# Four unused tiles between the buffers of a chunk's split activations

## The chip, the cores and the metric

The kernel runs on one core of a Trainium2 chip. The metric is device time in microseconds (us) for one execution, and the figure given for a kernel is the median of its runs. Five engines work side by side: TensorE (PE in the profile, with its weight loads listed apart as PEld), VectorE (DVE), ScalarE (ACT), GpSimd (POOL) and SyncE (SP), which issues DMAs. A tile on the chip has 128 partitions; where this text gives a tile's size or place in bytes, it means bytes in one partition.

## The reference

The reference is a light convolution followed by a feed-forward layer that keeps a maximum in place of an activation. `x` is (8, 4160, 192), the filters are (8, 4160, 8, 7), and the three up weights are (192, 768) each; the output has 33,280 rows of 192.

```python
w = exp(weight_gen - max); w = w / (sum(w) + 1e-9)       # over the 7 taps, for each head
x_unf = x_pad[:, s + k, :]                                # the last 7 rows up to s
attn = einsum('bshk,bskhg->bshg', w, x_unf)               # 8 heads of 24 columns
h = maximum(maximum(attn @ w1, attn @ w2), attn @ w3)     # 192 -> 768
out = h @ w_out                                           # 768 -> 192
```

Everything is float32 in the reference. The kernel multiplies tiles of type F32R on TensorE and keeps the precision by splitting each operand into a high part and a low part.

## The kernel before, in words

**Chunks and ticks.** The 33,280 rows are cut into 65 chunks of 512 (`TC` = 4 blocks of 128). A chunk takes 22 ticks of the main loop (L636 to L667). Ticks 0 to 11 are six up steps, ticks 12 to 15 are the down product of the chunk before, one block of 128 rows a tick, and ticks 16 to 21 are the last three up steps. Work for later chunks (loads, softmax, convolution, transpose, splitting) is put on a plan by tick (`PRODUCTS`, `SUMS`, `TRANSPOSE`, `PARTS`, `SOFTMAX`, `LOAD`, and for the first ticks `OPENING`). Every instruction is pinned in the order in which the code issues it (`pin`, L178), so the order on each engine is written out by hand.

**Convolution.** For each block, POOL multiplies 7 rows by their filters (L246), and DVE sums over the taps (L261). A chunk's 512 rows are then transposed: the first three chunks on TensorE (L276, L277), the others by DVE in blocks of 32 x 32 (L284) and 24 small copies on ACT (L290) into the tile `room`.

**Splitting the activations.** `parts` (L293) makes a chunk's four moving operands, all of 128 x 512 elements. Columns 0 to 127 of the 192 become `xa_hi` (ACT, L300) and the remainder `xa_lo` (POOL, or DVE for the first three chunks, L304). Columns 128 to 191 fill 64 partitions only, so `xc` holds their high part twice, once in each half of the partitions (ACT, L306), and `xb` holds the high part in partitions 0 to 63 (ACT, L308) and the low part in 64 to 127 (POOL or DVE, L309). These steps run at ticks 13 to 15 of the chunk before.

**Up product.** A step takes one of three weight matrices `i` and a pair `jp` of 128-column groups, first the even group and then the odd one (`odd`). The matmuls (L329) are cut into two halves of the partitions, 0 to 63 and 64 to 127, which TensorE works on together: each half has its own weight load and matmul, and a small model (`advance_upper`, L427) decides where the upper half's instructions go between the lower half's. Per half and step there are nine matmuls of 512 columns: `xa_hi`, `xa_lo` and again `xa_hi` with `wa_hi`, `wa_hi` and `wa_lo`, `xb` with `wb_hi`, for both groups, and `xc` with `wb_lo` for one of them. Nine steps make 81 matmuls per half and chunk.

**Maximum.** The first of the three results is copied by ACT from PSUM to `m` (L376), the others are compared by DVE (L378). ACT then makes `h_hi` (L381) and POOL `h_lo` (L385).

**Down product.** For each block of 128 rows and each of six groups `j`, the weights of TensorE are the slices of `h_hi` and `h_lo`, and the moving operand is `wo`: 384 columns (high and low part of `w_out`) with `h_hi`, then 192 columns with `h_lo`. That is 24 pairs per half and chunk. ACT and DVE add the two parts (L410, L411), and SP stores the chunk.

**Where tiles lie.** A pool lays its tiles out in the order in which each name is first asked for, all buffers of a name side by side, and the pools follow each other in the order of L155 to L161. Worked out from the tiles' sizes, with the place that the change's own words give for `xa_hi`, the tiles that matter here start as follows (modulo 2048):

| tile | bytes x buffers | start modulo 2048 |
|---|---|---|
| `wa_hi`, `wb_hi` | 9216 x 1 each | 640 |
| `wa_lo` | 9216 x 1 | 1664 |
| `wb_lo` | 4608 x 1 | 1664 |
| `wo` | 9216 x 1 | 128 |
| `room` | 9216 x 1 | 640 |
| `xa_hi`, `xa_lo`, `xb`, `xc` | 2048 x 2 each | 1664 |
| `h_hi`, `h_lo` | 12288 x 2 each | 1664 |
| `m` | 2048 x 4 | 1664 |
| `raw_a` (raw weights, opening) | 6144 x 1 | 1152 |

Slices `wa_hi[:, j, i]` that follow each other in `i` start 512 bytes apart, in `j` 1536 bytes apart; a slice of `h_hi` for one block of rows starts 512 bytes after the block before; a slice of `wo` starts 1536 bytes after the `j` before. During the opening the buffers of `h_hi` and `h_lo` also hold raw weights (L501 to L514), and `room` holds the raw `w_out` (L515).

Of the kernel before, what the change touches and what calls it, by code (L numbers as in the profile page):

```python
# [13 lines left out]
F32 = mybir.dt.float32  # L14
# [7 lines left out]
P = 128  # L22
# [76 lines left out]
def lightconv_maxout_kernel(  # L99
# [58 lines left out]
    xtp = ctx.enter_context(tc.tile_pool(name="xtp", bufs=2))  # L158
# [19 lines left out]
    def pin(ins):  # L178

        tc.keep_in_program_order(ins)  # L180
        return ins
# [111 lines left out]
    def parts(c):  # L293

        pa, pb = state.pop(("p", c))
        xa_hi = xtp.tile([P, CH], F32R, name="xa_hi")
        xa_lo = xtp.tile([P, CH], F32R, name="xa_lo")
        xb = xtp.tile([P, CH], F32R, name="xb")
        xc = xtp.tile([P, CH], F32R, name="xc")
        pin(nc.scalar.copy(xa_hi, pa))  # L300
        yield

        eng, at = (nc.vector, halves[0]) if c < ON_TENSOR else (nc.gpsimd, halves[1])
        pin(eng.tensor_tensor(xa_lo, pa, xa_hi.bitcast(F32), op=ALU.subtract))  # L304
        for h in halves:
            pin(nc.scalar.copy(xc[h], pb))  # L306
        yield
        pin(nc.scalar.copy(xb[:DB], xc[:DB].bitcast(F32)))  # L308
        pin(eng.tensor_tensor(xb[DB:], pb, xc[at].bitcast(F32), op=ALU.subtract))  # L309
        state["xT", c] = xa_hi, xa_lo, xb, xc  # L310
# [290 lines left out]
    def finish(name):  # L601
# [6 lines left out]
        "+": total,  # L608
        "t": transpose,
        "p": parts,  # L610
        "a": prepare_a,
        "b": prepare_b,
# [92 lines left out]
```

## Time and profile before

| what | value |
|---|---|
| median of 3 runs | 1697.91 us (1697.88 to 1699.43) |
| the profiled execution's own time | 1699.39 us |
| its span, first to last instruction | 1697.6 us |
| mean granted TensorE clock | 0.998 |
| busy: PE / PEld / DVE / ACT / POOL | 1657.2 / 1466.1 / 1124.6 / 1145.8 / 1426.2 us |
| HBM read / written | 51.25 / 25.56 MB |

A row of a group in the profile gives line, engine, operation, output `<-` inputs, shapes and count, then busy microseconds and mean nanoseconds of one instruction, then the engine's idle time just before such instructions with what ended it. In a timeline a row gives start and duration in us; "x2" means that two like instructions started there. The duration of a matmul includes its way through a pipeline and overlaps the next one, so the pace of matmuls is read from the distance of their starts.

### The profile page before, as it was taken

The page shows a single profiled execution, that of the slowest core. Times are in us where ns is not written, and L with a number is a line of the kernel's source. Part 1 is how long each engine was busy: PE and PEld are TensorE (multiplying, and loading weights), DVE is VectorE, ACT ScalarE, POOL GpSimd, SP SyncE. Part 2 cuts the span into 40 slices and gives each one's busy share as a digit, 9 for nine tenths or more (in the row PEclk, how much of TensorE's full clock was granted, in tenths as well). Part 3 has the DMA queues.
Part 4 walks back from the last instruction along what each step waited for, and adds up shares of the span by engine and source line. Part 5 has one row for each costly group of instructions (what it writes and reads, how often), then busy time and mean ns, then how long its engine had stood idle before and what let it go on. Part 6 is the DMA issues. An engine that isn't in the chain of part 4 may idle for free.

```text
span 1697.6 us, 42191 instructions
## 1 busy us (share of the span) xinstructions
PE 1657.2 (98%) x16794; PEld 1466.1 (86%) x16794; DVE 1124.6 (66%) x1552; ACT 1145.8 (67%) x2896; POOL 1426.2 (84%) x844
## 2 busy tenths in 40 slices
PE   3899999999999999999999999999999999999999
PEld 2598889889889889889988988988988988988998
DVE  7966766666666666666666666666666666666653
ACT  5657667667666766766766766766776776676672
POOL 6888888989888888888888888988888888888872
PEclk9999999999999999999999999999999999999999
DMA  7010101101010110101010110101011010101000
GB/s 236 1 70 10 70 29 52 70 20 60 20 70 15 66 70 21 60 21 70 11 70 21 60 70 20 61 20 70 11 70 61 27 63 20 70 11 46 20 11 29
DMA packets 20422, 79.51 MB, mean 47 GB/s; under 512 B 2320, under 2 KB 5128, under 8 KB 17536
## 3 DMA queue, kind: packets, MB, share of 16 engines
q1 hardware_dynamic: 20104, 76.54, 11.9%
q8 instruction: 131, 2.15, 0.5%
q14 instruction: 67, 0.55, 0.1%
q10 hardware_dynamic: 120, 0.28, 0.0%
HBM read 51.25 MB, written 25.56 MB: 45 GB/s over the span
## 4 chain that ended last, share of the span: by engine, by line
PE 94%; DVE 3%; ACT 1%; DMA 1%; POOL 1%; SPq 0%; issue 0%; DVEq 0%
PE ph L329 94%; DVE acc L261 1%; DVE m L378 0%; DMA wt<-in_weight_gen_dram 0%; DVE ph L483 0%; POOL r L246 0%; DVE ph L488 0%; DVE e L495 0%; DVE ph L481 0%; DVE ph L494 0%; DMA xt<-in_x_dram 0%; SPq L529 0%; ACT room L290 0%; SPq L521 0%; POOL h_lo L385 0%
## 5 line engine op out<-in xcount | busy, mean ns | idle before, releaser
L246 POOL TENSOR_TENSOR r<-xt,wt 128x1344 f32<-128x1344 f32 x260 | 721.4, 2814 | 0.6 <-DMA xt<-in_x_dram 0.4
L378 DVE TENSOR_TENSOR m<-ph,m 128x512 f32<-128x512 f32 x780 | 520.6, 685 | 197.4 <-PE ph L329 113.7
L329 PE MATMUL ph<-xa_hi,wa_hi 64*128 64x512 f32 x2340 | 630.8, 391 | 9.4 <-DVE m L378 3.1
L385 POOL TENSOR_TENSOR h_lo<-m,h_hi 128x512 fp32r<-128x512 f32 x390 | 503.3, 1301 | 161.7 <-ACT h_hi L381 157.0
L329 PE MATMUL ph<-xa_lo,wa_hi 64*128 64x512 f32 x2340 | 626.9, 388 | 1.0 <-DVE xa_lo L304 1.0
L329 PE MATMUL ph<-xa_hi,wa_lo 64*128 64x512 f32 x2340 | 626.1, 387 | 1.1 <-POOL wa_lo L498 1.1
L329 PE MATMUL ph<-xb,wb_hi 64*128 64x512 f32 x2340 | 626.0, 387 | 0.0
L329 PE MATMUL ph<-wo,h_hi 64*128 64x384 f32 x3120 | 595.5, 355 | 0.0
L329 PE MATMUL ph<-wo,h_lo 64*128 64x192 f32 x3120 | 522.3, 247 | 0.0
L381 ACT CAST h_hi<-m 128x512 fp32r<-128x512 f32 x390 | 241.8, 621 | 409.7 <-DVE m L378 406.6
L261 DVE TENSOR_REDUCE acc<-r 128x192 f32<-128x1344 f32 x260 | 401.8, 1547 | 125.5 <-POOL r L246 125.5
L290 ACT COPY room<-room 32x128 f32<-32x128 f32 x1488 | 440.8, 296 | 25.7 <-DVE room L284 7.5
L329 PE MATMUL ph<-xc,wb_lo 64*128 64x512 f32 x1170 | 453.1, 387 | 0.1
L329 PEld LDWEIGHTS ph<-wo,h_lo 64*128 64x128 f32 x3120 | 398.8, 188 | 2.5
L329 PEld LDWEIGHTS ph<-wo,h_hi 64*128 64x128 f32 x3120 | 398.4, 184 | 2.9 <-issue 0.4
L329 PEld LDWEIGHTS ph<-xa_hi,wa_hi 64*128 64x128 f32 x2340 | 338.7, 185 | 53.9 <-DVE m L378 3.9
L329 PEld LDWEIGHTS ph<-xa_hi,wa_lo 64*128 64x128 f32 x2340 | 338.4, 185 | 42.0 <-POOL wa_lo L498 1.5
L329 PEld LDWEIGHTS ph<-xa_lo,wa_hi 64*128 64x128 f32 x2340 | 338.7, 185 | 38.7 <-DVE xa_lo L304 1.5
L329 PEld LDWEIGHTS ph<-xb,wb_hi 64*128 64x128 f32 x2340 | 338.7, 185 | 38.4 <-ACT xb L308 0.3
L376 ACT COPY m<-ph 128x512 f32<-128x512 f32 x390 | 221.8, 586 | 38.5 <-PE ph L329 35.3
L411 DVE TENSOR_TENSOR o<-ph,ob 128x192 f32<-128x192 f32 x260 | 86.7, 353 | 234.5 <-ACT ob L410 234.5
L329 PEld LDWEIGHTS ph<-xc,wb_lo 64*128 64x128 f32 x1170 | 216.3, 185 | 20.9 <-POOL wb_lo L498 0.5
(54 smaller groups left out, 702.6 us busy)
## 6 DMA issues: line engine op xcount, KB each, us to landing
xt<-in_x_dram SPq DMA_DIRECT2D x20, 1728.0 KB, 7.1
out_dram<-o SPq DMA_DIRECT2D x64, 384.0 KB, 2.3
wt<-in_weight_gen_dram SPq DMA_DIRECT2D x21, 336.0 KB, 3.0
h_hi<-in_moe_w_dram SPq DMA_DIRECT2D x6, 256.0 KB, 4.8
xt<-in_x_dram SPq DMA_DIRECT2D x1, 1536.0 KB, 9.3
h_lo<-in_moe_w_dram SPq DMA_DIRECT2D x6, 192.0 KB, 4.8
room<-in_moe_w_out_dram SPq DMA_DIRECT2D x1, 1152.0 KB, 8.1
xt<-in_x_dram SPq DMA_DIRECT2D x1, 960.0 KB, 5.2
```

What stands on the lines that cost most here:

```text
L246: nc.gpsimd.tensor_tensor(r.rearrange("p (h g) k -> p k h g", g=G), xt[:, la + t : la + t + K].rearrange("p k (h g) -> p k h g", g=G), wt[ ...
L261: nc.vector.tensor_reduce(state["acc", c][:, t], r, axis=AX.X, op=ALU.add)
L290: pin(nc.scalar.copy(to[:, :, p : p + 32], blocks[p : p + 32, :, f : f + 32]))
L329: ins = nc.tensor.matmul(ph[:, :n], w[h], v[h], start=begins and half == 0 and q == 0, stop=ends and half == 1 and q == len(terms) - 1,)
L376: pin(nc.scalar.copy(m[:, :N], ph[:, :N]))
L378: pin(nc.vector.tensor_tensor(m[:, :N], ph[:, :N], m[:, :N], op=ALU.max))
L381: later(1, lambda: pin(nc.scalar.copy(hi, m[:, :N])))
L385: nc.gpsimd.tensor_tensor(lo, m[:, :N], hi.bitcast(F32), op=ALU.subtract)
L411: pin(nc.vector.tensor_tensor(o[:, t], po[:, :D], ob, op=ALU.add))
```

## The change

In `parts`, and for the first chunk only, four tiles are asked for that nothing writes or reads. They come from the same pool, one after each of the four operands:

```diff
         xa_hi = xtp.tile([P, CH], F32R, name="xa_hi")
+        if c == 0:
+            xtp.tile([P, 64], F32, name="gap0", bufs=1)
         xa_lo = xtp.tile([P, CH], F32R, name="xa_lo")
+        if c == 0:
+            xtp.tile([P, 80], F32, name="gap1", bufs=1)
         xb = xtp.tile([P, CH], F32R, name="xb")
+        if c == 0:
+            xtp.tile([P, 96], F32, name="gap2", bufs=1)
         xc = xtp.tile([P, CH], F32R, name="xc")
+        if c == 0:
+            xtp.tile([P, 16], F32, name="gap3", bufs=1)
         pin(nc.scalar.copy(xa_hi, pa))
```

The gaps are 256, 320, 384 and 64 bytes, each with one buffer. The starts of `xa_hi`, `xa_lo`, `xb` and `xc` modulo 2048 become 1664, 1920, 192 and 576, with both buffers of each name at the same one. All that is laid out behind them (`h_hi`, `h_lo`, `m`, `o`, `ob` and the tiles of the preparation) lies 1024 bytes further on. No instruction is added, removed or moved in the code.

## The prediction

> **What bounds the kernel now.** I read the page first, then the chain of waits, then TensorE's timeline. The page:
>
> ```profile
> span 1697.6 us, 42191 instructions
> ...
> PE 1657.2 (98%) x16794; PEld 1466.1 (86%) x16794; DVE 1124.6 (66%) x1552; ACT 1145.8 (67%) x2896; POOL 1426.2 (84%) x844
> ...
> PE 94%; DVE 3%; ACT 1%; DMA 1%; POOL 1%; SPq 0%; issue 0%; DVEq 0%
> ```
>
> TensorE's matmuls are the chain for 94% of the span. Busy shares alone would not prove that, since pipelined matmuls always look busy, so the chain in order of time and the busy time by stretch come next.
>
> ```profile
> 84.35 68.39 PE ph L329 x636
> ...
> 170.18 1523.98 PE ph L329 x14710
> ...
> 1694.19 0.33 ACT ob L410
> ```
>
> ```profile
> 170.00:424.00 254.00, 253.82 (x2596) 225.87 (x2598) 168.51 (x228) 175.28 (x447) 222.24 (x130) 1.00 0.13 50
> ...
> 1186.00:1440.00 254.00, 254.00 (x2602) 226.05 (x2600) 168.07 (x226) 175.17 (x448) 219.64 (x128) 1.00 0.11 42
> ```
>
> Up to 170 us the chain changes engines (weight splitting on DVE, a first run of matmuls, one late preparation). From 170.18 us to 1694.16 us it is one unbroken run of matmuls on L329, at a granted clock of 1.00. (Columns of the last two rows: stretch, length, then busy us of PE, PEld, DVE, ACT, POOL, clock, DMA share, GB/s.) POOL, the next busiest, is idle for 254.00 - 219.64 = 34.4 us of such a stretch, or 3.4 us a chunk.
>
> The chunk's length is read from the first down matmul of a chunk. It alone lasts 0.33 us, so it is easy to find:
>
> ```profile
> 184.61 0.33 PE L329 MATMUL ph<-wo,h_hi 64*128 64x384 f32 x1
> ...
> 209.80 0.33 PE L329 MATMUL ph<-wo,h_hi 64*128 64x384 f32 x1
> ...
> 1645.43 0.33 PE L329 MATMUL ph<-wo,h_hi 64*128 64x384 f32 x1
> ...
> 1670.62 0.33 PE L329 MATMUL ph<-wo,h_hi 64*128 64x384 f32 x1
> ```
>
> 209.80 - 184.61 = 25.19 us, 1670.62 - 1645.43 = 25.19 us, and (1670.62 - 184.61) / 59 chunks = 25.19 us. So all of them have one period. It splits into two rates:
>
> ```profile
> 801.13 0.39 PE L329 MATMUL ph<-xa_hi,wa_hi 64*128 64x512 f32 x2
> 801.36 0.39 PE L329 MATMUL ph<-xa_lo,wa_hi 64*128 64x512 f32 x2
> 801.58 0.39 PE L329 MATMUL ph<-xb,wb_hi 64*128 64x512 f32 x2
> 801.81 0.39 PE L329 MATMUL ph<-xa_hi,wa_lo 64*128 64x512 f32 x1
> ...
> 803.17 0.39 PE L329 MATMUL ph<-xa_hi,wa_hi 64*128 64x512 f32 x2
> ...
> 805.21 0.39 PE L329 MATMUL ph<-xa_hi,wa_hi 64*128 64x512 f32 x2
> ...
> 817.09 0.36 PE L329 MATMUL ph<-wo,h_hi 64*128 64x384 f32 x2
> 817.28 0.25 PE L329 MATMUL ph<-wo,h_lo 64*128 64x192 f32 x2
> 817.37 0.36 PE L329 MATMUL ph<-wo,h_hi 64*128 64x384 f32 x2
> ...
> 818.51 0.36 PE L329 MATMUL ph<-wo,h_hi 64*128 64x384 f32 x2
> ```
>
> "x2" means that both row halves started that matmul together. An up step is nine matmuls per half and takes 805.21 - 803.17 = 2.04 us, or 0.2267 us a matmul; the duration column (0.39) overlaps the next matmul and is not the pace. A down pair (384 and 192 columns) takes (818.51 - 817.09) / 5 = 0.284 us. Nine steps and 24 pairs are 9 x 2.04 + 24 x 0.284 = 25.18 us: the whole period, with nothing left for waits.
>
> **The change part by part.** The four `gap` tiles have no reader or writer. They add no instruction, wait or DMA, and the instructions that remain are pinned in program order. So the number of instructions stays 42191, and the only thing that can change a time is where tiles lie. Three groups move.
>
> First, the moving operands. Before, xa_hi, xa_lo, xb and xc all start at 1664 modulo 2048, since each buffer is 2048 bytes. After it xa_hi stays and the others start at 1920, 192 and 576. Their matmuls are these:
>
> ```profile
> L329 PE MATMUL ph<-xa_hi,wa_hi 64*128 64x512 f32 x2340 | 630.8, 391 | 9.4 <-DVE m L378 3.1 <-ACT xa_hi L300 2.8 <-DVE e L495 1.7
> L329 PE MATMUL ph<-xa_lo,wa_hi 64*128 64x512 f32 x2340 | 626.9, 388 | 1.0 <-DVE xa_lo L304 1.0
> L329 PE MATMUL ph<-xa_hi,wa_lo 64*128 64x512 f32 x2340 | 626.1, 387 | 1.1 <-POOL wa_lo L498 1.1
> L329 PE MATMUL ph<-xb,wb_hi 64*128 64x512 f32 x2340 | 626.0, 387 | 0.0
> ...
> L329 PE MATMUL ph<-xc,wb_lo 64*128 64x512 f32 x1170 | 453.1, 387 | 0.1
> ```
>
> Per half that is (4 x 2340 + 1170) / 2 = 5265 matmuls, 81 a chunk. One nanosecond on each would be 5.3 us. The trace already varies the places against each other. The weight slice of a step moves by 512 bytes with i and by 1536 with j, so its start goes through 640, 1152, 1664 and 128 modulo 2048 while the moving operand stays at 1664; step after step takes 2.04 us all the same. And while the lower half reads wo, whose slices lie 1536 bytes apart (128, 1664, 1152, 640), the upper half still reads xa_hi to xc:
>
> ```profile
> 814.45 0.25 PE L329 MATMUL ph<-wo,h_lo 64*128 64x192 f32 x1
> 814.51 0.39 PE L329 MATMUL ph<-xa_hi,wa_hi 64*128 64x512 f32 x1
> ...
> 816.32 0.39 PE L329 MATMUL ph<-xa_hi,wa_lo 64*128 64x512 f32 x1
> ```
>
> That is eight of the upper half's matmuls in 1.81 us, 0.226 us each, against 0.2267 us when both halves read the same place. So I take nothing for breaking up the common place. What the trace does not hold is a moving operand whose start is not 128 modulo 512; the new ones are 384, 192 and 64. That is the bound left open on both sides, priced under the rivals.
>
> Second, what ACT, DVE and POOL do on those tiles and on what lies behind them. The gaps add 256 + 320 + 384 + 64 = 1024 bytes, so h_hi and h_lo go from 1664 to 640, and m, o, ob and the preparation tiles shift by 1024 as well. h_hi's 512-byte slices pass through the same four starts as before.
>
> ```profile
> L381 ACT CAST h_hi<-m 128x512 fp32r<-128x512 f32 x390 | 241.8, 621 | 409.7 <-DVE m L378 406.6
> ...
> L300 ACT CAST xa_hi<-room 128x512 fp32r<-128x512 f32 x62 | 38.5, 621 | 1.5
> ...
> L385 POOL TENSOR_TENSOR h_lo<-m,h_hi 128x512 fp32r<-128x512 f32 x390 | 503.3, 1301 | 161.7 <-ACT h_hi L381 157.0
> ...
> L304 POOL TENSOR_TENSOR xa_lo<-room,xa_hi 128x512 fp32r<-128x512 f32 x62 | 80.5, 1298 | 25.2 <-ACT xa_hi L300 25.2
> ...
> L476 ACT COPY f<-h_hi 128x512 uint16<-128x512 uint16 x6 | 3.7, 613 | 0.0
> ...
> L476 ACT COPY f<-raw_a 128x512 uint16<-128x512 uint16 x3 | 1.8, 614 | 0.0
> ```
>
> The first pair reads from 1664 (m) and from 640 (room), 621 ns both; the second likewise, 1301 and 1298 ns; the third from 1664 (h_hi) and 1152 (raw_a), 613 and 614 ns. Three nanoseconds at most, so zero. What covers these steps if that is wrong:
>
> ```profile
> 797.65 1.29 POOL L309 TENSOR_TENSOR xb<-room,xc 64x512 fp32r<-64x512 f32 x1
> ...
> 802.49 0.39 PE L329 MATMUL ph<-xb,wb_hi 64*128 64x512 f32 x1
> ```
>
> The chunk starts six up steps before its first down matmul at 814.28 us, at 802.04 us, and reads xb third. xb was ready at 798.94 us, so 3.5 us of matmuls cover it. POOL's write would have to take nearly four times as long before TensorE waited; past that point every microsecond would be paid 65 times.
>
> Third, the opening. Weight splitting on DVE and ACT works from 1024 bytes further on, before 170 us, on the chain. At the 1 ns by which L476 differs between places, 18 splits of about nine operations are 0.2 us either way. The sum over all three is 0.0 us within 0.2.
>
> The Trainium skill speaks against any effect: its page "SBUF — State Buffer", section "Door 1: The DMA port swizzle (why `[64,N]` ≈ `[32,N]`)", has the banks that the compute engines see made of four partitions each, so an offset along the partition changes no bank. The constant 2.04 us agrees for the starts that occur here.
>
> The profiled execution took 1699.39 us, 1.8 us more than its span of 1697.6 and 1.5 us above the median of the three runs (1697.91, range 1.55). With a sum of zero, the profiled execution stays at 1699.4 and the median at 1697.9. I call 0.2%, 3.4 us, what can be told from no change.
>
> **The rivals.**
>
> *The four operands hinder each other at one place, and spreading them helps.* For it: all four do start at the same place, and in an up step the halves often read different ones of them. Against it: the rows at 814.51 and 816.32. The timeline shows the steps of 801.13 to 801.81 as 0.23, 0.22 and 0.23 us. If every matmul took the shorter value, a step would be 9 x 0.22 = 1.98 us, 0.06 less, and 9 x 65 steps would save 35 us: 1663 us. It decides from 3.4 / 5265 = 0.65 ns a matmul. "TensorE: Matmul & The Clock Gate", section "Back-to-back issue gap", in the Trainium skill gives N / 2.4 + 2.5 ns, which is 215.8 ns for 512 columns; an estimate with that pace would save 10.9 x 5265 = 57 us, or 1640 us, and nothing here shows such a pace.
>
> *xb and xc, now at odd multiples of 64 bytes, are read more slowly.* Every moving operand before starts at a multiple of 128 (1664 = 13 x 128); 192 and 576 do not. If such a start costs each matmul as much as the longer value shown, 0.23 against 0.2267 us, the 3.3 ns fall on (2340 + 1170) / 2 = 1755 matmuls per half: 5.8 us, 1703.7 us. It decides from 3.4 / 1755 = 1.9 ns a matmul. For it: no row has such a start, and in this chain nothing would hide it. Against it: nothing in the rows varies with a start at all.
>
> *The change doesn't do what it says.* An unused tile could be given no room, or lie elsewhere. Then the program is the one before, at 1697.9 us, which this trace can't tell from my forecast.
>
> **How the numbers follow.** No effect (with the third rival in it): 0.79. Helped by spreading: 0.11, as the halves and the weights contradict it, while starts other than 128 modulo 512 are untried. Hindered at odd multiples of 64: 0.10, the same gap in the rows seen from the other side. The forecast is 1697.9 us. Its own range is the 3.4 us on either side. The range given reaches to 1703.7 us, the second rival's price, and down to 1692.6 us, where 1 ns less per up matmul would lie; most of the first rival stays outside. Faster by over 0.2%: 0.11; within 0.2%: 0.79; slower: 0.10.
>
> **What would show it.** Right: 42191 instructions, first down matmuls 25.19 us apart, up steps of 2.04 us, the five matmul groups at 387 to 391 ns, L381 and L385 at 621 and 1301 ns, and the long run from about 170 us. The first rival shows as a step under 2.03 us with the down pairs still at 0.284; the second as a longer interval from the start of xb or xc to the next matmul alone, with xa_hi's unchanged. A preparation that came late would show as matmuls waiting for xb L309 or xa_lo L304 at chunk starts. A period other than 25.19 us with unchanged intervals would prove my reading of the bound wrong.

## The result, and the profile after

The changed kernel takes 1724.7 us (median of 4 runs, 1723.83 to 1725.83) against 1697.97 us for the kernel before in the same runs: ratio 1.0156, 95% interval 1.0138 to 1.0173. The forecast was no change. The profiled execution took 1725.83 us, 26.4 us more than the one before.

The page of the changed kernel, its chain of waits, and one row of busy time by stretch (the stretch whose row of before stands in the prediction):

```profile
span 1724.0 us, 42191 instructions
...
PE 1685.7 (98%) x16794; PEld 1649.6 (96%) x16794; DVE 1130.0 (66%) x1552; ACT 1149.1 (67%) x2896; POOL 1437.9 (83%) x844
...
PE 93%; DVE 3%; ACT 1%; POOL 1%; DMA 1%; issue 0%; SPq 0%; DVEq 0%; ACTq 0%; POOLq 0%
```

```profile
171.17 1549.44 PE ph L337 x13512
```

```profile
1186.00:1440.00 254.00, 254.00 (x2562) 253.98 (x2561) 166.04 (x221) 172.71 (x439) 217.87 (x126) 1.00 0.11 42
```

The number of instructions is the same, the chain is still one long run of matmuls (L329 is L337 now), and the granted clock is still 1.00. POOL and DVE are a little less busy per stretch. So nobody makes TensorE wait; it just starts 2562 matmuls in 254 us where it started 2602. The busy time of PEld, the time in which at least one weight load is on, went from 226.05 to 253.98 us, which fits halves whose loads no longer coincide (the rows marked x2 below show that they don't start together).

The first down matmuls of chunks, and then up steps and down pairs:

```profile
185.90 0.33 PE L337 MATMUL ph<-wo,h_hi 64*128 64x384 f32 x1
...
211.51 0.33 PE L337 MATMUL ph<-wo,h_hi 64*128 64x384 f32 x1
...
1697.08 0.33 PE L337 MATMUL ph<-wo,h_hi 64*128 64x384 f32 x1
```

```profile
471.57 0.39 PE L337 MATMUL ph<-wo,h_hi 64*128 64x384 f32 x2
...
472.99 0.39 PE L337 MATMUL ph<-wo,h_hi 64*128 64x384 f32 x2
...
479.74 0.46 PE L337 MATMUL ph<-xa_hi,wa_hi 64*128 64x512 f32 x2
479.96 0.46 PE L337 MATMUL ph<-xa_lo,wa_hi 64*128 64x512 f32 x2
480.19 0.47 PE L337 MATMUL ph<-xb,wb_hi 64*128 64x512 f32 x2
480.43 0.39 PE L337 MATMUL ph<-xc,wb_lo 64*128 64x512 f32 x1
...
481.82 0.46 PE L337 MATMUL ph<-xa_hi,wa_hi 64*128 64x512 f32 x2
```

The period of a chunk is (1697.08 - 185.90) / 59 = 25.61 us, 0.43 more than before, and again the same from chunk to chunk (211.51 - 185.90 = 25.61). Five down pairs still take 1.42 us, 0.284 each. The up step takes 481.82 - 479.74 = 2.08 us instead of 2.04; over the period it is 2.04 + 0.43 / 9 = 2.087. Between the two 59-chunk marks that is 1511.18 - 1486.01 = 25.2 of the 26.4 us, and the first mark is 1.3 us later than before. The rows marked x2 show a second thing: they last 0.46 or 0.47 instead of 0.39 us, since they join two matmuls that start 0.07 to 0.08 us apart. Before, the halves started together.

The five groups of up matmuls, and the two groups on ACT and POOL that the prediction compared:

```profile
L337 PE MATMUL ph<-xb,wb_hi 64*128 64x512 f32 x2340 | 632.1, 394 | 0.0
L337 PE MATMUL ph<-xa_hi,wa_lo 64*128 64x512 f32 x2340 | 632.0, 393 | 0.0
L337 PE MATMUL ph<-xa_hi,wa_hi 64*128 64x512 f32 x2340 | 630.7, 394 | 8.5 <-ACT xa_hi L308 2.8 <-DVE m L386 2.5 <-DVE e L503 1.6
L337 PE MATMUL ph<-xa_lo,wa_hi 64*128 64x512 f32 x2340 | 628.8, 390 | 1.0 <-DVE xa_lo L312 1.0
...
L393 POOL TENSOR_TENSOR h_lo<-m,h_hi 128x512 fp32r<-128x512 f32 x390 | 505.8, 1311 | 178.0 <-ACT h_hi L389 173.2
...
L337 PE MATMUL ph<-xc,wb_lo 64*128 64x512 f32 x1170 | 459.9, 393 | 0.1
...
L389 ACT CAST h_hi<-m 128x512 fp32r<-128x512 f32 x390 | 241.8, 621 | 401.5 <-DVE m L386 398.3
```

All five groups grew by 2 to 7 ns, that of xa_hi too (391 and 387 to 394 and 393), though xa_hi has not moved. ACT and POOL hardly changed (621 and 1311 ns against 621 and 1301).

### The profile page after: what moved, and what is told of

It is laid out like the page before. It is cut to its first block, busy times and chain, and to the rows that moved or that the text cites. A ratio compares the mean times of both kernels' runs of the same rounds, so it can differ in the third digit from the quotient of the medians.

```text
span 1724.0 us, 42191 instructions
## 1 busy us (share of the span) xinstructions
PE 1685.7 (98%) x16794; PEld 1649.6 (96%) x16794; DVE 1130.0 (66%) x1552; ACT 1149.1 (67%) x2896; POOL 1437.9 (83%) x844
## 4 chain that ended last, share of the span: by engine, by line
PE 93%; DVE 3%; ACT 1%; POOL 1%; DMA 1%; issue 0%; SPq 0%; DVEq 0%; ACTq 0%; POOLq 0%
PE ph L337 93%; DVE acc L261 1%; POOL r L246 0%; ACT room L290 0%; DVE m L386 0%; DMA wt<-in_weight_gen_dram 0%; DVE ph L491 0%; DVE ph L496 0%; DVE e L503 0%; DVE ph L502 0%; DVE ph L489 0%; POOL h_lo L393 0%; ACT m L384 0%; SPq L537 0%; DMA xt<-in_x_dram 0%
## 5 line engine op out<-in xcount | busy, mean ns | idle before, releaser
L246 POOL TENSOR_TENSOR r<-xt,wt 128x1344 f32<-128x1344 f32 x260 | 731.9, 2861 | 0.7 <-DMA xt<-in_x_dram 0.5
L393 POOL TENSOR_TENSOR h_lo<-m,h_hi 128x512 fp32r<-128x512 f32 x390 | 505.8, 1311 | 178.0 <-ACT h_hi L389 173.2
L337 PE MATMUL ph<-xa_hi,wa_hi 64*128 64x512 f32 x2340 | 630.7, 394 | 8.5 <-ACT xa_hi L308 2.8
L337 PE MATMUL ph<-xb,wb_hi 64*128 64x512 f32 x2340 | 632.1, 394 | 0.0
L337 PE MATMUL ph<-xa_hi,wa_lo 64*128 64x512 f32 x2340 | 632.0, 393 | 0.0
L337 PE MATMUL ph<-xa_lo,wa_hi 64*128 64x512 f32 x2340 | 628.8, 390 | 1.0 <-DVE xa_lo L312 1.0
L337 PE MATMUL ph<-wo,h_hi 64*128 64x384 f32 x3120 | 590.6, 355 | 0.0
L337 PE MATMUL ph<-wo,h_lo 64*128 64x192 f32 x3120 | 546.0, 247 | 0.0
L337 PEld LDWEIGHTS ph<-wo,h_lo 64*128 64x128 f32 x3120 | 467.9, 188 | 0.1
L337 PEld LDWEIGHTS ph<-wo,h_hi 64*128 64x128 f32 x3120 | 462.3, 184 | 0.6 <-issue 0.6
L337 PE MATMUL ph<-xc,wb_lo 64*128 64x512 f32 x1170 | 459.9, 393 | 0.1
L337 PEld LDWEIGHTS ph<-xa_hi,wa_hi 64*128 64x128 f32 x2340 | 367.2, 185 | 19.4 <-ACT xa_hi L308 3.3
L337 PEld LDWEIGHTS ph<-xa_hi,wa_lo 64*128 64x128 f32 x2340 | 362.3, 185 | 6.2 <-POOL wa_lo L506 0.4
L337 PEld LDWEIGHTS ph<-xb,wb_hi 64*128 64x128 f32 x2340 | 359.0, 185 | 6.1 <-ACT xb L316 0.3
L337 PEld LDWEIGHTS ph<-xa_lo,wa_hi 64*128 64x128 f32 x2340 | 352.5, 185 | 6.3 <-DVE xa_lo L312 1.5
L337 PEld LDWEIGHTS ph<-xc,wb_lo 64*128 64x128 f32 x1170 | 217.4, 186 | 3.4 <-POOL wb_lo L506 0.5
```

What stands on the lines that cost most here:

```text
L246: nc.gpsimd.tensor_tensor(r.rearrange("p (h g) k -> p k h g", g=G), xt[:, la + t : la + t + K].rearrange("p k (h g) -> p k h g", g=G), wt[ ...
L337: ins = nc.tensor.matmul(ph[:, :n], w[h], v[h], start=begins and half == 0 and q == 0, stop=ends and half == 1 and q == len(terms) - 1,)
L393: nc.gpsimd.tensor_tensor(lo, m[:, :N], hi.bitcast(F32), op=ALU.subtract)
```

## Experiments

Theories at the start: **A**, a row half pays when its next moving operand starts elsewhere than the last one; **B**, a start that is not 128 modulo 512 is read more slowly; **C**, the time comes from what lies behind the four operands.

### What lies behind, one common place, steps of 512

The first, second and third kernel, each with unused tiles in `parts` as in the change, the rest being the kernel before:

```diff
# e1_behind_only
         xc = xtp.tile([P, CH], F32R, name="xc")
+        if c == 0:
+            xtp.tile([P, 256], F32, name="gap3", bufs=1)
# e2_all_at_576
+        if c == 0:
+            xtp.tile([P, 240], F32, name="pre", bufs=1)
         xa_hi = xtp.tile([P, CH], F32R, name="xa_hi")
...
         xc = xtp.tile([P, CH], F32R, name="xc")
+        if c == 0:
+            xtp.tile([P, 16], F32, name="gap3", bufs=1)
# e3_steps_of_512: as the change, with four gaps of [P, 128]
```

> One unused tile of 1024 bytes behind xc: the four operands stay at 1664 modulo 2048, and all that lies behind them moves by 1024 bytes as in the changed kernel. Theory A (a row half pays when its next moving operand does not start where the last one did, modulo some power of two): no change, 1698 us, up step 2.04 us. Theory B (a moving operand whose start is not 128 modulo 512, or an odd multiple of 64, is read more slowly): 1698 us. Theory C (h_hi, h_lo, m and the others at their new places cost the time): 1724.7 us, up step 2.087 us.

> An unused tile of 960 bytes ahead of xa_hi and one of 64 behind xc: all four operands at 576 modulo 2048, an odd multiple of 64, and the rest at the places of the changed kernel. Theory A: no change, 1698 us, up step 2.04 us, since all four still start at one place. Theory B: slower than the changed kernel, as xa_hi and xa_lo are now off as well: 47 ns a step fell on at most five of nine matmuls there, so 9/5 of it, 85 ns a step, 1748 us. Theory C: 1724.7 us.

> Four unused tiles of 512 bytes: xa_hi, xa_lo, xb, xc at 1664, 128, 640, 1152 modulo 2048, the rest at 1664 as before. Theory A with modulus 1024 or 2048: slower, about 1725 us. Theory A with a modulus that divides 512: no change, 1698 us. Theory B: no change, 1698 us, since all starts are 128 modulo 512. Theory C: no change, 1698 us.

Measured: e1 1698.86 us, ratio 1.000 (0.9991 to 1.001). e2 1731.4 us, ratio 1.0192 (1.0176 to 1.0207). e3 1698.18 us, ratio 0.9996 (0.9986 to 1.0006). C falls with e1. A falls with e2, where all four start at one place and the kernel is slower than the changed one. e3 is free, as B has it. B's direction holds; its size for e2 (1748 us) was too large, 32 us (1731.4 - 1698.94) in place of 50. In the timeline of e2:

```profile
800.19 0.39 PE L333 MATMUL ph<-xa_hi,wa_lo 64*128 64x512 f32 x2
800.42 0.40 PE L333 MATMUL ph<-xa_hi,wa_hi 64*128 64x512 f32 x2
...
802.29 0.39 PE L333 MATMUL ph<-xa_hi,wa_lo 64*128 64x512 f32 x2
```

The step is 2.10 us, and the x2 rows last 0.39 and 0.40 us: here the halves stay together and still lose the time. So the time is lost without the halves falling out of step.

### A placement for each chunk

One tile of 8192 bytes and some room holds all four operands, and each chunk has its own offsets in it, so that one run times a placement in each of 59 chunks:

```diff
-        xa_hi = xtp.tile([P, CH], F32R, name="xa_hi")
-        xa_lo = xtp.tile([P, CH], F32R, name="xa_lo")
-        xb = xtp.tile([P, CH], F32R, name="xb")
-        xc = xtp.tile([P, CH], F32R, name="xc")
+        x4 = xtp.tile([P, 4 * CH + 704], F32R, name="x4")
+        xa_hi, xa_lo, xb, xc = (x4[:, o : o + CH] for o in PLACES.get(c, HOME))
```

> The four operands of a chunk are slices of one larger tile with two buffers, and each chunk from 5 to 63 has places of its own; the trace gives one up step time per placement. References at one common place: 2.04 us by every theory; the changed kernel's places (chunks 6 and 63): 2.087 us. All four shifted together by 16 to 320 bytes (chunks 7 to 12): A 2.04 us, B over 2.04 us at 16, 32, 64 and 320. xa_lo alone shifted by d (chunks 13 to 39): A depends on d alone and is 2.04 us again at multiples of the modulus; B is 2.04 us at 512, 1024 and 1536 and the same at d and d + 512. xb alone and xc alone (chunks 41 to 54): A less for xc, which half the groups read, B in proportion to their share, 2/9 and 1/9 of the matmuls.

The up step is read as the distance of a half's xc matmuls (one a step). In this trace, chunk 22 (xa_lo alone 256 bytes further) and chunk 41 (xb alone 64 bytes further):

```profile
609.08 0.39 PE L396 MATMUL ph<-x,wb_lo 64*128 64x512 f32 x1
...
611.12 0.39 PE L396 MATMUL ph<-x,wb_lo 64*128 64x512 f32 x1
...
1092.47 0.39 PE L396 MATMUL ph<-x,wb_lo 64*128 64x512 f32 x1
...
1094.55 0.39 PE L396 MATMUL ph<-x,wb_lo 64*128 64x512 f32 x1
```

2.04 us in the first, 2.08 in the second. The same reading for the others, in us a step (median of the steps ahead of the down product; two values are those of the lower and the upper half, where they are more than 5 ns apart):

| shift against 1664, bytes | all four | xa_hi alone | xa_lo alone | xb alone | xc alone |
|---|---|---|---|---|---|
| 0 | 2.040 | 2.040 | 2.040 | 2.040 | 2.040 |
| 16 | 2.086 | | 2.087 | | |
| 32 | 2.100 | | 2.088, 2.082 | | |
| 64 | 2.060 | 2.087, 2.080 | 2.090 | 2.090 | 2.087 |
| 128 | 2.090 | | 2.053 | 2.054, 2.080 | 2.047 |
| 256 | 2.040 | 2.040 | 2.040 | 2.040 | 2.040 |
| 512, 1024 and 1536 | | 2.040 (1024) | 2.040 | 2.040 | 2.040 |

Every multiple of 256 is free, for xa_lo also 768, 1280 and 1792, and no other shift that was tried is. So B needs 256 in place of 512, and it is not about odd multiples of 64. The changed kernel's own places gave 2.086. The whole run took 1709.66 us.

The values off the multiples are not firm, since a half can have either of two paces at one placement. With xa_lo at 128 and 1152 both halves take 2.053 us a step. At 640 and at 384 (chunk 24) the lower half takes 2.053 and the upper half 2.080, side by side. Two xc matmuls of the lower half, three steps apart, and two of the upper half in chunk 24:

```profile
659.89 0.39 PE L396 MATMUL ph<-x,wb_lo 64*128 64x512 f32 x1
660.62 0.39 PE L396 MATMUL ph<-x,wb_lo 64*128 64x512 f32 x1
...
666.05 0.39 PE L396 MATMUL ph<-x,wb_lo 64*128 64x512 f32 x1
666.86 0.39 PE L396 MATMUL ph<-x,wb_lo 64*128 64x512 f32 x1
```

That is (666.05 - 659.89) / 3 = 2.053 us and (666.86 - 660.62) / 3 = 2.080 us. In chunk 42 (xb at 128) the lower half takes 2.054 ahead of its down product and 2.085 behind it, so the pace also depends on what came before.

### The weights' place

In the kernel before all weights start at 128 modulo 256, as the operands do. Whether 128 is good in itself (**P**), whether the distance to the weights counts (**R**), or whether a multiple of 256 would be better than both (**L**) needs the weights moved. Unused tiles of the pool `const`, and for e7 the sweep with the weights moved:

```diff
# e5_all_by_128
+    const.tile([P, 32], F32, name="pad0")
     ident = const.tile([P, P], F32, name="ident")
# e6_weights_by_128 (e7: pad2 of [P, 32], and the sweep)
     ident = const.tile([P, P], F32, name="ident")
+    const.tile([P, 32], F32, name="pad1")
     wa_hi = const.tile([P, NJ, 3, P], F32R, name="wa_hi")
...
     wo = const.tile([P, NJ, 2 * D], F32R, name="wo")
+    const.tile([P, 480], F32, name="pad2")
```

> An unused tile of 128 bytes ahead of everything, so that all tiles keep their distances and every start that was 128 modulo 256 is 0 modulo 256. Theory R (what counts is the moving operand's start against the weights' start, modulo 256): no change, 1698 us, up step 2.04 us. Theory P (what counts is the moving operand's own start modulo 256, and 128 is the good one): as with the four operands at 0 modulo 256 in the sweep, 2.09 us a step, 9 x 0.05 x 65 = 29 us more, 1727 us. Theory L (a row of 2048 bytes that starts at 128 modulo 256 touches nine blocks of 256 bytes, one that starts at 0 eight, and a block is what is paid for): faster, at best 8/9 of 2.04 us a step, 1.81 us, 1565 us.

> The weights (wa_hi, wa_lo, wb_hi, wb_lo, wo) lie 128 bytes further on, at 0 modulo 256; the four operands, h_hi and h_lo stay at 128 modulo 256. Theory R: slower, 1727 us, up step 2.09 us, and the down pairs (wo moves there, h_hi and h_lo are the weights) slower too if they have no room left. Theory P: up step 2.04 us, 1698 us but for the down pairs, where wo is the moving operand. Theory L: up step 2.04 us.

> The sweep again with the weights at 0 modulo 256, a placement a chunk from chunk 5 on. Theory R: an up step is 2.04 us where the four operands are at 0 modulo 256 (chunks 6, 12) and 2.09 us where they are at 128 (chunks 5, 7). Theory P: the other way round, 2.04 us at 128 and 2.09 us at 0. Theory L: under 2.04 us at 0. One operand alone off by 64 costs about 47 ns a step by each of them.

Measured: e5 1698.09 us, ratio 0.9994 (0.9985 to 1.0004). e6 1730.67 us, ratio 1.0184 (1.0167 to 1.0201). Two xc matmuls of one half, a step apart, in e5 and then in e6:

```profile
904.85 0.39 PE L330 MATMUL ph<-xc,wb_lo 64*128 64x512 f32 x1
...
906.89 0.39 PE L330 MATMUL ph<-xc,wb_lo 64*128 64x512 f32 x1
```

```profile
904.84 0.39 PE L331 MATMUL ph<-xc,wb_lo 64*128 64x512 f32 x1
...
906.93 0.39 PE L331 MATMUL ph<-xc,wb_lo 64*128 64x512 f32 x1
```

2.04 and 2.09 us. In e6 no moving operand of the up product has moved, and it is about as slow as e2. The same xc matmul comes again 25.71 us later, a chunk on, 0.53 more than before; the steps account for 9 x 0.05 = 0.45 of it, and the rest lies at the down product, where wo has moved too. The sweep turns round with the weights; chunk 6 (all four at 0 modulo 256) and chunk 7 (all four at 128) of e7:

```profile
203.94 0.39 PE L398 MATMUL ph<-x,wb_lo 64*128 64x512 f32 x1
...
205.98 0.39 PE L398 MATMUL ph<-x,wb_lo 64*128 64x512 f32 x1
...
229.34 0.39 PE L398 MATMUL ph<-x,wb_lo 64*128 64x512 f32 x1
...
231.43 0.40 PE L398 MATMUL ph<-x,wb_lo 64*128 64x512 f32 x1
```

2.04 us at 0, 2.09 us at 128, and so in the 23 other chunks of the 59 that have all four at 0 or all four at 128 (2.04 us in nine, 2.09 to 2.10 in fourteen). R holds; P and L fall. Nothing in either sweep was under 2.04 us. The whole run of e7 took 1725.66 us.

### The change put right, and its parts

> The changed kernel with xb moved by 64 bytes down and xc by 64 up: gaps of 256, 256 and 512 bytes, starts 1664, 1920, 128, 640, all 128 modulo 256; the rest lies as in the changed kernel. By theories R, P and L: up step 2.04 us, 1698 us. If spreading over several places costs by itself: near 1724.7 us.

e8 has gaps of `[P, 64]`, `[P, 64]` and `[P, 128]` behind xa_hi, xa_lo and xb, and takes 1698.63 us, ratio 1.0001 (0.9992 to 1.001). Spreading the operands neither costs nor gains anything as long as the steps are multiples of 256.

> The changed kernel with xc put right alone: xa_hi, xa_lo, xb, xc at 1664, 1920, 192, 640; xb (two of nine matmuls a step) is the only operand off 128 modulo 256. Theory S (an operand that is off costs its own matmuls, and the costs add): two thirds of the change's 26.7 us, 1698 + 18 = 1716 us, with the extra time at the xb matmuls alone. Theory F (one operand that is off upsets the whole stream, the matmuls of the others too, and two do no more than one): 1725 us, up step near 2.087 us.

> The changed kernel with xb put right alone: starts 1664, 1920, 128, 576; xc (one of nine matmuls a step) is the only operand off 128 modulo 256. Theory S: one third of 26.7 us, 1698 + 9 = 1707 us. Theory F: 1725 us, up step near 2.087 us.

e9 has gaps of 256, 320 and 448 bytes, e10 of 256, 256, 448 and 64. e9: 1726.03 us, ratio 1.0158 (1.0143 to 1.0174). e10: 1715.01 us, ratio 1.0093 (1.0078 to 1.0108). A step of e9, then one of e10:

```profile
909.11 0.39 PE L335 MATMUL ph<-xc,wb_lo 64*128 64x512 f32 x1
...
911.19 0.40 PE L335 MATMUL ph<-xc,wb_lo 64*128 64x512 f32 x1
```

```profile
908.22 0.39 PE L337 MATMUL ph<-xc,wb_lo 64*128 64x512 f32 x1
...
909.61 0.39 PE L337 MATMUL ph<-xa_hi,wa_hi 64*128 64x512 f32 x1
...
910.29 0.39 PE L337 MATMUL ph<-xc,wb_lo 64*128 64x512 f32 x1
```

So xb alone costs all that the change costs, xc alone 15.6 us (1715.01 - 1699.40), and both together no more than xb. F (one is as bad as two) holds for xb and not for xc; S (the costs add) fails for both.

The rows of e10 show more. The extra time is not spread over the step: the six matmul distances from xc on take 909.61 - 908.22 = 1.39 us in place of 6 x 0.2267 = 1.36, and the last three 910.29 - 909.61 = 0.68, as before. Averaged over the trace, the nine distances are 0.2333, 0.2258, 0.2358, 0.2283, 0.2325, 0.2308 and three times 0.2267 us, the same in both halves, each counted from its own xc. So an operand that is off slows some of the matmuls behind it too, those of operands in place included, and six matmuls later the pace is the old one. xc comes once in nine matmuls, xb every four or five: with xb off, the next one comes before the stream has recovered. That fits that xb and xc together cost no more than xb.

> The four operands stay at 1664 as before; the weight wb_lo alone (one of nine weight loads a step, the one for xc) lies 64 bytes further on, at 192 modulo 256, and the rest keeps its place. Theory R (the moving operands' starts against the weights' starts, modulo 256): slower although no moving operand has moved; with theory F near 1725 us, with S near 1707 us. Theory P (the moving operand's own start alone): 1698 us.

```diff
+    const.tile([P, 16], F32, name="pad1")
     wb_lo = const.tile([P, NJ // 2, 3, P], F32R, name="wb_lo")
+    const.tile([P, 496], F32, name="pad2")
```

1719.97 us, ratio 1.0125 (1.0108 to 1.0142). One weight of nine a step, off by 64 with all moving operands in place, costs 20.6 us (1719.97 - 1699.40): between the 9 and the 27 us expected, and far from P's zero. The first down matmuls of two chunks, with two xc matmuls of one half, a step apart, between them:

```profile
923.59 0.33 PE L331 MATMUL ph<-wo,h_hi 64*128 64x384 f32 x1
...
939.05 0.39 PE L331 MATMUL ph<-xc,wb_lo 64*128 64x512 f32 x1
...
941.11 0.39 PE L331 MATMUL ph<-xc,wb_lo 64*128 64x512 f32 x1
...
949.13 0.33 PE L331 MATMUL ph<-wo,h_hi 64*128 64x384 f32 x1
```

The period is 25.54 us, 0.35 more than before, but the step is only 2.06 us. So 9 x 0.02 = 0.18 us a chunk lies in the steps, and the other half of the cost lies where the down product runs, though wo has kept its place; why is open.

### One half alone

To tell whether the two reads meet within a half or between the halves, the upper half is left out, with the places of before (e12) and of the change (e13):

```diff
     def product_of(ph, terms, half, key, begins=True, ends=True):
+        if half == 1:
+            state.pop(("begun", key), None)
+            for n, _, _ in terms:
+                yield SLOTS[n]
+            return
...
-                stop=ends and half == 1 and q == len(terms) - 1,
+                stop=ends and q == len(terms) - 1,
```

> Leaves out all matmuls and weight loads of the upper row half (partitions 64 to 127), so the sums lack those rows; places as in the kernel before. Theory W (the cost lies within a half, between its own weight loads and its own moving operand): up step of the lower half 2.04 us as with both halves. Theory H (the cost lies between the halves): 2.04 us or less. It is the reference for the next run.

> The same with the places of the changed kernel (1664, 1920, 192, 576); it leaves out the matmuls and weight loads of the upper half too. Theory W: the lower half alone is slower than in the run before it by about 47 ns a step, 2.087 us if that was 2.04, and the whole by about 27 us. Theory H: same step and same time as in the run before it.

Measured: 3120.71 us and 3120.50 us, against 1698.43 for the kernel before. The timelines of e12 and e13:

```profile
1500.10 0.62 PE L335 MATMUL ph<-xa_hi,wa_hi 64*128 64x512 f32 x1
1500.10 0.33 PEld L335 LDWEIGHTS ph<-xa_lo,wa_hi 64*128 64x128 f32 x1
1500.52 0.62 PE L335 MATMUL ph<-xa_lo,wa_hi 64*128 64x512 f32 x1
```

```profile
1500.28 0.62 PE L343 MATMUL ph<-xa_lo,wa_hi 64*128 64x512 f32 x1
1500.71 0.62 PE L343 MATMUL ph<-xb,wb_hi 64*128 64x512 f32 x1
```

A half alone starts a matmul every 0.42 to 0.43 us, nearly twice 0.2267, with both placements. The two agree, as theory H has it, but at a pace at which either read has nearly twice the time, so this decides nothing. No theory had foreseen the pace. Two traces with both halves say more: in e10 each half shows the same series of distances behind its own xc, and in chunk 24 of e4 the halves keep two paces while they drift against each other. Both speak for a cost within each half.

## Why the prediction was wrong

**The bound** was read rightly. The period is nine up steps and 24 down pairs with nothing between, before and after; that is why 47 ns a step came through undamped as 0.43 us a chunk (9 x 0.0474) and 26.4 us in all.

**"The trace already varies the places against each other"** is the step that failed. The weight slices do pass through four starts, but 512 or 1536 bytes apart, and wo's too; h_hi's are 512 apart. All of these are multiples of 256, so every pair of weight and moving operand in the trace before had one and the same distance modulo 256, namely zero. The trace held no test of what the change does. The prediction saw half of it ("what the trace does not hold is a moving operand whose start is not 128 modulo 512") and still put 0.79 on no effect, as though absence of variation were evidence. The runs showed in its place that multiples of 256 bytes cost nothing (e3, e8) and that xb and xc, off by 64 and 192 modulo 256, cost 47 ns a step.

**The second rival** named the right operands and the right direction, in part by luck: with these four gaps, the two operands at odd multiples of 64 are also the two that are off modulo 256. It was mis-sized and too narrow. Its price, 3.3 ns on 1755 matmuls, 5.8 us, came from a row of 0.23 us beside a mean of 0.2267, which is the rounding of the timeline and no measure of any read. Measured: 47 ns a step, 5.2 ns a matmul on average over the nine of a half, those of the operands in place included (e10 shows how unevenly); 26.4 us on the span. The sign that it gave, a longer interval behind xb and xc alone with that of xa_hi unchanged, did not come either (e10). Its rule, odd multiples of 64, was wrong: 128 costs as well, and what counts is the distance to the weights (e6, e11).

**The first rival** fell: spreading by itself does nothing (e8, e3). **The second and third groups** of moved tiles cost nothing, as forecast (e1). After the opening no matmul waited for xb or xa_lo, so the preparation's cover held.

**The banks.** The prediction also argued from the Trainium skill, page "SBUF — State Buffer", section "Door 1: The DMA port swizzle (why `[64,N]` ≈ `[32,N]`)": the banks that the compute engines see consist of four partitions each. From this it concluded that an offset along the partition changes nothing. That conclusion does not hold here: such an offset changed the time by 1.6%, and the measurement decides.

**What stays open.** A moving operand and a weight that differ modulo 256 slow the stream; that is shown from both sides. How they do it is not. One reading is that the weight load for the next matmul and the read of the current operand, which run at the same time, get in each other's way. e11 speaks against its simplest form: there wb_lo is loaded while xb is read, and the distance from xb to xc stays 0.226 us; the longer one, 0.236, comes behind xc, the matmul whose own weight and operand differ. That the cost arises within a half is supported by e10 and chunk 24 of e4, but not tested by itself. Why it carries over to the matmuls that follow, why its size depends on the distance and on what came before, and why e11 pays at the down product were not settled.

## What to carry to other kernels

For matmuls like these (F32R, 512 columns, two row halves; no other kind was tried), where TensorE runs with no slack, place weights and moving operands so that their starts in a partition are equal modulo 256 bytes; a small tile in a pool (or a new constant) can shift all that follows, and a slowdown then shows as a slightly longer distance of matmul starts with no wait to explain it. When a trace is taken as proof that something doesn't matter, check that the values it holds differ in the way that the change would make them differ.

## What the runs showed of the hardware that was not expected

- Up matmuls of 512 columns start every 0.2267 us with operands and weights equal modulo 256 bytes, whatever the multiple and wherever both lie (e3, e5, e8); with one or all of them off, a step of nine took between 2.047 and 2.11 us instead of 2.040.
- One operand that was off slowed each half for six matmul distances, 1.39 us in place of 1.36, and then the old pace was back (e10). The two halves could run side by side at 2.053 and 2.080 us a step (e4).
- The 32 us of e2 and e6 (1.9% and 1.8%) were the most that any placement cost in a whole kernel.
- One row half alone ran its matmuls 0.43 us apart and its weight loads in 0.33 us, where both halves together had 0.2267 and 0.185, while the granted clock in the records was 1.00. Leaving out half of the matmuls made the kernel 1.84 times as long.
